# The last feed-forward groups of a two-layer transformer on one core: 256, 128 and 128 tokens in place of 384 and 128

## The chip, the core and the metric

The kernel runs on one core of a Trainium2 chip. A core has engines that work side by side and wait for each other by semaphores: TensorE (PE; its weight loads are listed as PEld), VectorE (DVE), ScalarE (ACT), GpSimd (POOL) and SyncE (SP, which here only issues DMAs). PE writes to PSUM, eight banks of 128 x 512 float32 values; ACT and DVE read PSUM, POOL does not. The metric is the device time of one execution, in microseconds (us).

## The reference

Two identical layers, same weights, over 2048 tokens of width 512; 32 heads of width 16; the feed-forward part is 1792 wide. All inputs and the output are bfloat16.

```python
def _A_ref(x, wqkv, wo):
    q, k, v = split((x @ wqkv), 3, heads=32)             # 32 heads of 16
    scores = einsum("bhqd,bhkd->bhqk", q, k) * 16 ** -0.5
    o = einsum("bhqk,bhkd->bhqd", softmax(scores), v)
    return o.reshape(B, S, D) @ wo
def _B_ref(x, w_gate, w_up, w_down):
    return (gelu_tanh(x @ w_gate) * (x @ w_up)) @ w_down

x = A_x
for layer in (0, 1):
    x = x + _A_ref(layernorm(x), A_wqkv, A_wo)
    x = x + _B_ref(layernorm(x), B_w_gate, B_w_up, B_w_down)
```

(The reference writes the four steps out one after the other, and the head split with a transpose.)

## The kernel before

**Work.** The tokens of a layer are cut into query blocks, `layer_blocks`: four of 512 in layer 0; 512, 512, 512, 256, 128 and 128 in layer 1. A *unit* is one block with one group of four heads; there are 80, each gone through twice.

The *first pass* makes the scores of 128 queries with 512 keys of one head in a PSUM bank (PE, L1791) and DVE reduces one or two banks at once to row maxima (L1806). Some of this is *folded*: PE scores the queries with the difference of two key blocks (L1610), ACT keeps its positive part (L1617), and one special DVE instruction adds the plain scores and takes the maximum (L1801), so that one DVE instruction does two tiles.

The *second pass* makes the scores again with the keys as rows (PE, L1661), with the maximum taken away by a row that four small DMAs put beside the queries (L1189); ACT takes exponentials of one or two banks at once into `SCR` (L1637); PE multiplies them with the values (L1685) into bank 7; ACT copies that out (L1238), POOL or DVE divides by the row sum. A *position* is two tiles of 512 columns of either pass; each pass has 2048 positions over both layers.

After a block's second pass comes its output projection, `outproj`, whose result ACT copies (L1266) for POOL to add to `X` (L1268), or DVE adds at once (L1261). Then the feed-forward part (FFN), `ffn`, for one *group* of tokens, `ffn_groups`: four of 512 in layer 0; 512, 512, 512, 384 and 128 in layer 1. It normalises the group's tokens and turns each 128-token tile by a DMA on SP's queue (L921), then goes through three stages:

- gates: for each of 14 slices of 128 columns, four matmuls as wide as the group (L717), and a gelu on ACT into `HT` (L1353). From the first gate to the last `gel["on"]` is set (L1348 to L1356): no exponential is given out in that time, since gelu and exponential need different ACT tables (`ACT_TABLE_LOAD`); below it is called the *pause*. The first pass goes on in it.
- up-projection: 14 times four matmuls, and the product with `HT`, either by DVE alone (L1363) or by a copy on ACT (L1369) and a product on POOL (L1371).
- down-projection: for each tile of 128 tokens 14 matmuls of 512 columns, then in layer 1 the sum with `X` on DVE (L1389) and a DMA to the output.

The groups hold the buffer `HT` one after another (`locks`). The last group, of 128 tokens, has a name of its own, `HTL`, for the columns from `c0` on (L1319), and takes a *fast* way: its vector work goes to DVE, its transposes through PE, and its gelu table is loaded ahead of its layer norm (L1326). It can only start after the last unit's second pass.

**Order.** No engine decides anything while the kernel runs. A planner in `_build` writes the order of every engine's instructions when the kernel is built. It keeps an estimated clock per engine; tasks such as `outproj` or `ffn` are generators with a due position of the first pass; the main loop at each step gives PE a first-pass tile or pair, second-pass tiles, a PV product, a piece of a task, or, if PE's recent load is low, a filler matmul with zeros (L1830). Semaphore waits are added afterwards from the buffers read and written.

A group's FFN becomes open when its first tile is projected, its gates need all its tiles normalised, and its due position is the end of the block that holds its last token, less 10 (`FDL`; the last group is urgent, L1470 to L1474).

**Constants.** `PLAN` has 132 rows; row k holds for the 16 positions of the first pass from 16k on (L1847). There are 2048 positions, so row 128 holds after the first pass's end, and rows 129 to 131 are never read. The names of the 21 numbers of a row stand in the same line:

```python
SPC, SPLIT, S1C, S2C, OV, LIM, NT, P2B, LAG, LAGT, FL, GL, FX, AHD, DUE, DUEM, PIECE, GP, NPV, PB, OVF = PLAN[stretch[0]]
```

Those that matter most below: `LAGT`: a result is evacuated from PSUM by DVE if the first pass is more than that many positions ahead of the second, else by ACT (`pick`; after the first pass's end always by DVE). `P2B`: which bank pairs the second pass may use in ordinary mode; with 0 none, so that exponentials are single tiles. In *wide* mode pairs are always used; near the end (first pass beyond position 1688) the mode is wide when the second pass is over 10 positions behind and no task piece is open or ready with a due position that has come. After the first pass pairs are used anyway. `S1C`, `S2C`, `SPC`, `SPLIT`, `LIM`, `OV`, `OVF`: when the next pass tile must be given out and how far other work may push it back. `PIECE`, `GP`: how many matmuls of a task, or of a gate, form one piece, counted in 512 columns. `NT`: second-pass tiles given out at once. `DUE`, `DUEM`, `AHD`: what counts as due and as ready.

The lines that the mode and the pairs hang on:

```python
wide = pos["p1"] - pos["p2"] > (LAGE if near_end() else LAG) and not opened and can_p2[0] and not (fresh and min(c.due for c in fresh) < pos["p1"] + DUE)
for b in ((0, 2, 4) if pos["g"] >= len(p1_list) else (3, 5) if wide else ((), (4,), (4, 5))[P2B]):
```

Of the kernel before, what the change touches and what calls it, by code (L numbers as in the profile page):

```python
# [153 lines left out]
]  # L154


# [157 lines left out]
            self.done = True  # L314


def _build(nc, x_in, wqkv, wo, wg, wu, wd, out, layer_blocks=((512, 512, 512, 512), (512, 512, 512, 256, 128, 128)), ffn_groups=((512, 512, 512, 512), (512, 512, 512, 384, 128)),
           n_ahead=6, n_pre=6, S1C=0.45, S2C=0.42, OV=0.3, PD=80, FDUE=20, LIM=-0.05, NT=1, AHD=2.0, DUEM=2, FDL2=0, OPD=12, URG=0.3, ft_tok=512, n_pt=8, n_qt=8, SPLIT=0.15, SPC=0.1, PVC=47, WARM=0.55, WARML=0.42, NPV=7, BOOST=0.0, LAG=62, LAGT=84, GP=2, SING=0, DUE=0, END=360, LAGE=10, FD=205, FDL=-10, QD=32, KD_=16, VD=20, FL=8, FMAX=6, NKD=2, FLOOK=2, FX=0.3, GF=1, NSPL=5, HSPL=0, TSPL=1, HNA=3, TNA=3, PB=1, OVF=0.0, FNP=1, NSG=3, LNT=8, HV=16, TW=0.95, HF=60, VS=14, SO=1.0, SF=1, SP=0, FAST=1, P2B=1, PIECE=2, GL=60, GLE=20, HARD=-1e9, VPARK=60, RUSH=1, XL=1000, NFE=2, NFA=6, LM1=0, T0=0.6, A3=1, DTX=2, DTA=2, T_TP=0.7, T_TPI=2.0, VL=0):
    S = x_in.shape[1]
    D = x_in.shape[2]  # L320
# [13 lines left out]
    with es:  # L334
# [980 lines left out]
        def ffn(la, t0, n, due):  # L1315
            tts = list(range(t0 // 128, (t0 + n) // 128))
            last = la == NL - 1
            fast = FAST and last and t0 + n == S
            c0 = ffn_groups[la][-2] if fast and ffn_groups[la][-2] + n <= ft_tok else 0  # L1319
            hn = "HTL" if c0 else "HT"  # L1320
            yield ("cond", lambda: ao_rec.get(tts[0]) == la)
            while locks.get(hn):
# [118 lines left out]
        for la in range(NL):  # L1441
# [28 lines left out]
            for gi, n in enumerate(ffn_groups[la]):  # L1470
                bi = [i for i, b in enumerate(blocks) if b[0] == la and b[2] <= f0 + n - 1 < b[2] + b[3]][0]
                lastb = gi == len(ffn_groups[la]) - 1
                due = URGENT if lastb and la == NL - 1 else blk_end[bi] + (FDL2 if lastb else FDL if la == NL - 1 else FD)
                add(ffn(la, f0, n, due), due)  # L1474
                f0 += n
# [598 lines left out]
```

## Time and profile before

| what | value |
|---|---|
| median of 3 runs | 2481.18 us (2481.1 to 2481.72) |
| the profiled execution | 2481.77 us, span 2480.0 us |
| granted TensorE clock | 1.00 |
| ACT_TABLE_LOAD at L1353 and at L1637 | 8 and 8, 1283 ns each |
| last tile of the first pass (L1806) ends | 2426.9 us |
| last exponential (L1637) ends | 2459.0 us |

The profile is one execution. Its page gives the busy time of each engine and the chain of work that ended last, followed back from the end; the trace answers further questions: instructions in order of time, groups of instructions in a window (count, busy time, mean of one in ns, idle time of the engine before them and who ended it), and the busy time of every engine in given stretches, where (x n) is the number of instructions. "SCR<-PS" names what is written and what is read. Times in the trace count from the span's start. An instruction's recorded duration overlaps the next one's start a little, so what it costs an engine in a row of its kind is the length of the row divided by the count.

### The profile page before, as it was taken

Reading aid. Unit: us, or ns where it says so; the run is one execution under the profiler, and the core shown is the slowest. Engines: PE = TensorE matmul, PEld = TensorE weight load, DVE = VectorE, ACT = ScalarE, POOL = GpSimd, SP = SyncE. Lnnn points to the kernel's source line nnn. Section 1 sums busy time; section 2 is a strip of 40 time slices with the busy share of each in tenths; the row PEclk is TensorE's granted clock in tenths of the full one; section 3 lists DMA queues with packets and bytes.
Section 4 is the critical chain, followed back from the end, with each engine's and each line's share of the span. In section 5 each row is a group of like instructions: output and inputs, shape, how many; then the busy total and the mean of one; then the engine's idle time right before and its main releaser. Section 6 shows DMA issues by size and latency. Waiting matters only on the chain.

```text
span 2480.0 us, 69071 instructions
## 1 busy us (share of the span) xinstructions
PE 2409.1 (97%) x30004; PEld 1147.4 (46%) x30004; DVE 2382.1 (96%) x3173; ACT 2331.1 (94%) x3415; POOL 810.2 (33%) x1311
## 2 busy tenths in 40 slices
PE   8999999999999999999999999999999999999999
PEld 3444444444434454344434444434544345544655
DVE  8999999999999999999998999999999999999993
ACT  7999998999989999899989999989999999978987
POOL 5121125425433353521333131623116321333520
PEclk9999999999999999999999999999999999999999
DMA  3110000000000001000000000000000000000000
GB/s 94 44 57 15 2 15 12 2 2 15 13 12 2 4 11 23 6 14 11 11 10 2 9 15 5 10 16 8 4 13 15 2 10 3 14 10 12 13 8 10
DMA packets 64816, 34.32 MB, mean 14 GB/s; under 512 B 46848, under 2 KB 63488, under 8 KB 64512
## 3 DMA queue, kind: packets, MB, share of 16 engines
q1 hardware_dynamic: 64512, 29.90, 5.2%
q8 instruction: 235, 3.85, 0.6%
q14 instruction: 69, 0.57, 0.1%
HBM read 10.22 MB, written 2.10 MB: 5 GB/s over the span
## 4 chain that ended last, share of the span: by engine, by line
PE 47%; DVE 33%; ACT 19%; issue 1%; POOL 0%; ACTq 0%
DVE PM L1806 31%; ACT SCR L1637 17%; PE PS L1791 16%; PE PS L717 13%; PE PS L1685 10%; PE PS L1661 4%; PE PS L1830 4%; DVE SCR L1801 1%; ACT SCR L1617 1%; PE PS L1610 0%; PE PS L914 0%; ACT AO L1266 0%; ACT ACCS L1238 0%; ACT L1637 0%; DVE ST L769 0%
## 5 line engine op out<-in xcount | busy, mean ns | idle before, releaser
L1806 DVE TENSOR_REDUCE PM<-PS 128x1 f32<-128x512 f32 (+1 forms) x2507 | 2189.9, 935 | 47.6 <-PE PS L1661 25.1
L1637 ACT ACTIVATE SCR<-PS 128x512 bf16<-128x512 f32 (+1 forms) x2726 | 2005.9, 848 | 45.9 <-PE PS L1661 32.2
L1791 PE MATMUL PS<-KT,QT 32*128 32x512 bf16 x3894 | 1019.3, 384 | 41.3 <-DVE PM L1806 25.2
L1661 PE MATMUL PS<-QT,KT 32*128 32x512 bf16 (+2 forms) x5120 | 919.3, 340 | 2.6 <-ACT SCR L1637 1.7
L1685 PE MATMUL PS<-VP,SCR 128*128 128x51 bf16 (+1 forms) x16384 | 802.9, 187 | 10.1 <-ACT SCR L1637 5.3
L1685 PEld LDWEIGHTS PS<-VP,SCR 128*128 128x128 bf16 x16384 | 574.7, 96 | 473.4 <-issue 395.6
L1791 PEld LDWEIGHTS PS<-KT,QT 32*128 32x128 bf16 x3894 | 243.2, 91 | 526.3 <-DVE PM L1806 298.2
L1830 PE MATMUL PS<-WV,ZER 128*128 128x240 bf16 x2284 | 419.9, 265 | 3.9 <-ACT ACCS L1238 1.9
L1248 POOL TENSOR_TENSOR RL<-ACCS,CM 128x16 f32<-128x16 f32 (+2 forms) x71 | 182.2, 2567 | 485.2 <-ACT ACCS L1238 484.6
L1661 PEld LDWEIGHTS PS<-QT,KT 32*128 32x128 bf16 x5120 | 247.6, 91 | 73.9 <-ACT SCR L1637 44.3
L1830 PEld LDWEIGHTS PS<-WV,ZER 128*128 128x128 bf16 x2284 | 170.0, 96 | 70.0 <-issue 57.3
L1145 POOL TENSOR_TENSOR PM<-PM 128x16 f32<-128x16 f32 (+3 forms) x142 | 32.4, 228 | 425.0 <-DVE PM L1806 410.7
L1371 POOL TENSOR_TENSOR HT<-HT,AO 128x512 bf16<-128x512 bf16 x91 | 105.4, 1161 | 174.0 <-ACT AO L1369 174.0
L1408 POOL TENSOR_TENSOR KD<-KT 128x512 bf16<-128x512 bf16 x80 | 92.2, 1153 | 139.6 <-PE PS L1610 132.8
L1617 ACT ACTIVATE SCR<-PS 128x512 bf16<-128x512 f32 (+1 forms) x143 | 112.1, 787 | 26.3 <-PE PS L1610 25.3
L1801 DVE CUSTOM_DVE_ANT_0 SCR<-PS,SCR 128x512 bf16<-128x512 f32 x202 | 130.1, 686 | 3.2 <-PE PS L1661 1.2
L717 PE MATMUL PS<-XNT,WU 128*128 128x512 bf16 (+2 forms) x504 | 132.2, 357 | 0.0
L717 PE MATMUL PS<-WD,HT 128*128 128x512 bf16 x448 | 130.7, 381 | 0.0
L1268 POOL TENSOR_TENSOR X<-X,AO 128x512 f32<-128x512 f32 x47 | 59.5, 1266 | 199.2 <-ACT AO L1266 199.2
L717 PE MATMUL PS<-XNT,WG 128*128 128x512 bf16 (+2 forms) x504 | 119.9, 358 | 0.7 <-ACT HT L1353 0.7
L1353 ACT ACTIVATE HT<-PS 128x512 bf16<-128x512 f32 (+2 forms) x126 | 68.5, 550 | 43.1 <-PE PS L717 42.3
L717 PEld LDWEIGHTS PS<-XNT,WG 128*128 128x128 bf16 x504 | 37.6, 97 | 57.8 <-issue 33.2
(128 smaller groups left out, 1043.0 us busy)
## 6 DMA issues: line engine op xcount, KB each, us to landing
KT<-SG SPq DMA_DIRECT2D x64, 64.0 KB
QT<-MT SPq DMA_DIRECT2D x244, 1.0 KB
QT<-SG SPq DMA_DIRECT2D x56, 64.0 KB
out_dram<-AO SPq DMA_DIRECT2D x16, 128.0 KB, 1.7
WG<-in_B_w_gate_dram SPq DMA_DIRECT2D x4, 448.0 KB, 5.1
WU<-in_B_w_up_dram SPq DMA_DIRECT2D x4, 448.0 KB, 4.8
WD<-in_B_w_down_dram SPq DMA_DIRECT2D x4, 384.0 KB, 4.6
QT<-MT SPq DMA_DIRECT2D x68, 0.2 KB
```

The source lines that it names most:

```text
L717: ins = e.matmul(out_ap, lhsT=l, rhs=r_, start=(i == 0), stop=(i == n - 1))
L1248: emit("pool", lambda e: e.tensor_tensor(RL[:, s, 0:4 * nq], lsum, AP(CM1, 0, [[1, 128], [0, 4 * nq]]), op=ALU.pow), r=[("ACCS", s), ("CM1 ...
L1371: emit("pool", lambda e, ft=ft, o=o: e.tensor_tensor(HT[:, ft, c0:c0 + n], HT[:, ft, c0:c0 + n], AO[:, o, 0:n], op=ALU.mult), r=[("AO", o) ...
L1408: emit("pool", lambda e: e.tensor_tensor(KD[:, s, :], KT[:, g, ka * 512:(ka + 1) * 512], KT[:, g, kb * 512:(kb + 1) * 512], op=ALU.subtrac ...
L1617: emit("act", lambda e: e.activation(PT[:, s0:s0 + cnt, :], PS[:, bk:bk + cnt, :], ACTF.Relu), r=bks, w=[("PT", s0 + d) for d in range(cnt ...
L1637: emit("act", lambda e: e.activation(dst, src, ACTF.Exp, scale=DH ** -0.5), r=[BK[bk + i] for i in range(cnt)], w=[("PT", i) for i in slot ...
L1661: ins = e.matmul(bank(bk)[:, i * n:(i + 1) * n], lhsT=KT[32 * j:32 * j + 32, g, kt * 128:(kt + 1) * 128], rhs=QT[32 * j:32 * j + 32, s, 0: ...
L1685: ins = e.matmul(acc, lhsT=PT[:, slot, i * n + qt * 128:i * n + (qt + 1) * 128], rhs=AP(VP, (kt * H + 4 * g + j) * 17, [[NTT * H * 17, 128 ...
L1791: ins = e.matmul(bank(b), lhsT=QT[32 * j:32 * j + 32, s, qt * 128:(qt + 1) * 128], rhs=KT[32 * j:32 * j + 32, g, kb * 512:(kb + 1) * 512], ...
L1801: emit("dve", lambda e, i=i, b=b, sl=sl: e.tensor_tensor_reduce(PT[:, sl, :], bank(b), PT[:, sl, :], 1.0, -3.0e38, ALU.add, ALU.max, po[:, ...
L1806: emit("dve", lambda e: e.tensor_reduce(po, PS[:, bs[0]:bs[0] + cnt, :], axis=AX.X, op=ALU.max), r=bks, w=[("PM", sm) + h[1:] for h in hs] ...
L1830: return e.matmul(PS[:, b, NACC:512], lhsT=ZER[:, :], rhs=WV[:, 0, 0:512 - NACC], start=(b != 7), stop=(b != 7), skip_group_check=True)
```

## The change

Two things. In layer 1 the FFN group of 384 tokens (1536 to 1919) becomes two, of 256 (1536 to 1791) and 128 (1792 to 1919). Both still use `HT` one after the other; the last 128 tokens are a fast group as before, and the line that gives its first column `c0` is written otherwise (512 - 128 = 384; before, the preceding group's 384). The due position of the 256 group is 1920 - 10, that of the middle 128 group 1984 - 10, as that of the 384 group was.

And 39 of PLAN's 132 rows, 93 to 131, have new numbers; they hold from position 1488 of the first pass on, which is from about 1743 us. Rows 0 to 92 and every default of `_build` but `ffn_groups` stay. A few of the rows, with their number at the end of the line here:

```diff
@@ PLAN @@
-    (0.4, 0.1, 0.55, 0.52, 0.0, -0.05, 3, 0, 70, 76, -2, 80, 0.7, 2.0, 10, 2, 2, 1, 7, 3, -0.1),      99
+    (0.2, 0.1, 0.75, 0.42, 0.0, 0.0, 2, 2, 70, 76, -2, 80, 0.7, 1.0, 10, 2, 2, 1, 7, 3, 0.1),         99
...
-    (0.3, 0.1, 0.55, 0.52, 0.5, -0.05, 2, 0, 30, 20, -17, 50, 0.4, 2.5, -10, 2, 1, 1, 14, 2, 0.0),    114
+    (0.3, 0.05, 0.55, 0.52, 0.5, -0.05, 2, 2, 30, 20, 8, 50, 0.4, 2.5, -10, 14, 1, 1, 14, 1, 0.0),    114
...
-    (0.1, 0.3, 0.45, 0.42, 0.1, 0.0, 2, 1, 14, 116, 13, 100, 0.3, 3.5, 0, 2, 2, 1, 7, 1, -0.05),      116
-    (0.15, 0.1, 0.55, 0.42, 0.3, -0.05, 2, 0, 22, 84, 13, 20, 0.3, 4.0, 0, 6, 2, 4, 9, 2, 0.0),       117
-    (0.15, 0.1, 0.45, 0.42, 0.3, -0.05, 2, 0, 22, 10, 8, 20, 0.3, 4.0, 0, 6, 2, 4, 9, 2, 0.0),        118
-    (0.35, 0.05, 0.55, 0.42, 0.2, -0.1, 2, 0, 22, 76, 8, 100, -0.2, 3.0, 0, 10, 1, 1, 11, 1, 0.1),    119
-    (0.15, 0.1, 0.45, 0.12, 0.5, 0.0, 2, 0, 22, 10, 8, 20, 0.3, 4.0, 0, 10, 1, 4, 9, 2, 0.2),         120
-    (0.2, 0.1, 0.55, 0.42, 0.3, -0.05, 2, 1, 22, 84, 8, 20, 0.4, 4.0, 0, 6, 2, 4, 14, 2, 0.0),        121
-    (0.2, 0.1, 0.55, 0.32, 0.3, -0.05, 2, 0, 22, 84, 8, 20, 0.3, 4.0, 10, 6, 2, 4, 5, 2, 0.2),        122
-    (0.35, 0.05, 0.65, 0.42, 0.2, -0.05, 2, 0, 62, 76, 8, 100, -0.3, 4.0, -5, -14, 1, 1, 11, 1, 0.1), 123
-    (0.35, 0.05, 0.55, 0.42, 0.7, -0.05, 2, 0, 62, 84, 8, 100, -0.3, 2.5, 20, 6, 1, 4, 11, 1, 0.0),   124
-    (0.35, 0.05, 0.55, 0.42, 0.2, -0.05, 2, 0, 62, 84, -2, 100, -0.3, 2.5, 20, 6, 1, 4, 11, 1, 0.05), 125
-    (0.3, 0.15, 0.75, 0.42, 0.3, -0.05, 3, 0, 5, 76, 8, 60, -0.2, 1.5, 15, -6, 2, 4, 14, 2, 0.0),     126
-    (0.3, 0.15, 0.75, 0.42, 0.0, -0.1, 2, 0, 14, 0, 8, 60, -0.3, 1.5, -10, -14, 2, 4, 3, 3, -0.05),   127
-    (0.2, 0.05, 0.65, 0.42, 0.3, -0.05, 1, 1, 30, 116, 8, 40, 0.7, 3.0, 15, 10, 1, 4, 14, 3, -0.1),   128
+    (0.15, 0.1, 0.55, 0.42, 0.3, -0.05, 2, 1, 30, 84, 8, 20, 0.3, 4.0, 0, 6, 2, 4, 9, 2, 0.0),        116
+    (0.15, 0.1, 0.55, 0.42, 0.3, -0.05, 2, 0, 70, 84, 8, 20, 0.3, 4.0, 0, 6, 2, 4, 9, 2, 0.0),        117
+    (0.15, 0.1, 0.15, 0.42, 0.3, -0.05, 2, 0, 22, 10, 8, 20, 0.2, 4.0, 0, 6, 2, 4, 9, 2, 0.0),        118
+    (0.15, 0.1, 0.15, 0.42, 0.3, -0.05, 2, 0, 22, 10, 8, 20, 0.2, 4.0, 0, 6, 2, 4, 9, 2, 0.0),        119
+    (0.15, 0.1, 0.15, 0.42, 0.3, -0.05, 2, 0, 22, 10, 13, 20, 0.2, 4.0, 0, 6, 2, 4, 9, 2, 0.0),       120
+    (0.2, 0.0, 0.65, 0.42, 0.3, -0.1, 2, 2, 70, 84, 8, 0, 0.3, 2.5, -5, 2, 2, 1, 7, 4, 0.1),          121
+    (0.3, 0.3, 0.55, 0.42, 0.1, 0.0, 3, 0, 22, 76, -30, 50, -0.3, 1.0, -5, -6, 2, 3, 3, 2, 0.2),      122
+    (0.15, 0.1, 0.45, 0.22, 0.0, -0.05, 2, 2, 70, 84, 8, 100, 0.2, 1.0, 0, 6, 2, 3, 9, 1, 0.0),       123
+    (0.35, 0.15, 0.75, 0.62, 0.3, -0.05, 3, 0, 5, 84, 8, 80, 0.3, 1.0, 15, -6, 2, 3, 3, 1, 0.0),      124
+    (0.3, 0.15, 0.75, 0.42, 0.3, -0.05, 3, 0, 5, 76, -2, 60, -0.2, 1.5, 15, -6, 2, 4, 14, 2, 0.0),    125
+    (0.05, 0.15, 0.75, 0.42, 0.1, -0.1, 3, 1, 14, 10, 13, 60, -0.3, 1.0, -10, -14, 1, 4, 3, 3, -0.05),126
+    (0.35, 0.05, 0.55, 0.52, 0.5, -0.05, 2, 0, 30, 20, 8, 50, 0.4, 2.5, -10, 2, 1, 1, 14, 2, 0.0),    127
+    (0.35, 0.05, 0.55, 0.52, 0.5, -0.05, 2, 0, 30, 20, 8, 50, 0.4, 2.5, -10, 2, 1, 1, 14, 2, 0.0),    128
...
@@ def _build @@
-  ffn_groups=((512, 512, 512, 512), (512, 512, 512, 384, 128)),
+  ffn_groups=((512, 512, 512, 512), (512, 512, 512, 256, 128, 128)),
...
@@ def ffn @@
-            c0 = ffn_groups[la][-2] if fast and ffn_groups[la][-2] + n <= ft_tok else 0
+            c0 = ft_tok - n if fast else 0
```

Among the new rows, P2B is 2 in rows 99, 111 to 114, 121 and 123 and 1 in rows 93, 116 and 126; before it was 1 in rows 116, 121 and 128 and 0 in the others from 93 to 127. LAGT is 40 or less in the new rows 93 to 96, 114, 118 to 120 and 126 to 128; before in 93, 103, 111, 112, 114, 118, 120 and 127.

More of the change, by code (lines that the diff above doesn't have):

```diff
@@ L314, in step, with _build @@
             self.done = True
-def _build(nc, x_in, wqkv, wo, wg, wu, wd, out, layer_blocks=((512, 512, 512, 512), (512, 512, 512, 256, 128, 128)), ffn_groups=((512, 512, 512, 512), (512, 512, 512, 384, 128)),
+def _build(nc, x_in, wqkv, wo, wg, wu, wd, out, layer_blocks=((512, 512, 512, 512), (512, 512, 512, 256, 128, 128)), ffn_groups=((512, 512, 512, 512), (512, 512, 512, 256, 128, 128)),
            n_ahead=6, n_pre=6, S1C=0.45, S2C=0.42, OV=0.3, PD=80, FDUE=20, LIM=-0.05, NT=1, AHD=2.0, DUEM=2, FDL2=0, OPD=12, URG=0.3, ft_tok=512, n_pt=8, n_qt=8, SPLIT=0.15, SPC=0.1, PVC=47, WARM=0.55, WARML=0.42, NPV=7, BOOST=0.0, LAG=62, LAGT=84, GP=2, SING=0, DUE=0, END=360, LAGE=10, FD=205, FDL=-10, QD=32, KD_=16, VD=20, FL=8, FMAX=6, NKD=2, FLOOK=2, FX=0.3, GF=1, NSPL=5, HSPL=0, TSPL=1, HNA=3, TNA=3, PB=1, OVF=0.0, FNP=1, NSG=3, LNT=8, HV=16, TW=0.95, HF=60, VS=14, SO=1.0, SF=1, SP=0, FAST=1, P2B=1, PIECE=2, GL=60, GLE=20, HARD=-1e9, VPARK=60, RUSH=1, XL=1000, NFE=2, NFA=6, LM1=0, T0=0.6, A3=1, DTX=2, DTA=2, T_TP=0.7, T_TPI=2.0, VL=0):
```

78 rows, old and new, of the table PLAN are left out of this document.

## The prediction

> **What bounds the kernel now.** I read the page first, then the chain of waits near the end, then the stretches between the last two feed-forward (FFN) groups, then the counts of instructions in them. The page:
>
> ```profile
> span 2480.0 us, 69071 instructions
> PE 2409.1 (97%) x30004; PEld 1147.4 (46%) x30004; DVE 2382.1 (96%) x3173; ACT 2331.1 (94%) x3415; POOL 810.2 (33%) x1311
> PE 47%; DVE 33%; ACT 19%; issue 1%; POOL 0%; ACTq 0%
> ```
>
> DVE and ACT are both nearly full, so an average decides nothing; the end does. The chain's last pieces, and four stretches (length, then busy PE, PEld, DVE, ACT, POOL; the first is used far below):
>
> ```profile
> 2410.74 0.32 PE PS L1791 x2
> 2411.06 0.76 PE PS L717 x4
> ...
> 2438.32 6.38 ACT SCR L1637 x7
> ...
> 2461.13 5.61 PE PS L717 x26
> ...
> 2467.71 9.40 PE PS L717 x126
> ```
>
> ```profile
> 1290.00:1380.00 90.00, 89.21 (x991) 37.20 (x990) 80.24 (x110) 86.01 (x160) 30.59 (x36) 1.00 0.03 6
> 2203.26:2400.91 197.65, 190.68 (x3166) 107.82 (x3164) 189.11 (x242) 188.75 (x304) 78.88 (x161) 1.00 0.05 10
> 2400.91:2419.67 18.76, 18.23 (x113) 7.52 (x113) 18.23 (x24) 9.44 (x16) 0.29 (x1) 1.00 0.01 1
> 2427.00:2459.00 32.00, 31.84 (x583) 19.51 (x582) 7.23 (x18) 31.72 (x44) 1.33 (x5) 1.00 0.01 3
> ```
>
> From 2427 to 2459 ACT works without a gap at exponentials, while DVE, whose first pass is over, stands idle for 24.8 of 32 us. What is left to ACT there:
>
> ```profile
> L1637 ACT ACTIVATE SCR<-PS 128x1024 bf16<-128x1024 f32 x30 | 28.8, 1042 | 0.1
> L1637 ACT ACTIVATE SCR<-PS 128x512 bf16<-128x512 f32 x8 | 4.8, 624 | 0.2 <-PE PS L1661 0.2
> ```
>
> A position of either pass is two 512-column tiles, so 30 + 8/2 = 34 positions stand between the passes. After them a tail of 21 us (last output projection, layer norm, last 128-token FFN) goes through PE. So the end is: ACT's last exponential, plus 21 us. What the change adds to ACT's way there is paid in full; DVE has room.
>
> The row 2400.91:2419.67 is the pause: the gelus of the 384-token group hold the exponentials up from one table load to the other, 18.76 us in which ACT is busy for 9.44.
>
> **The change part by part.** Its time comes from ACT's stream:
>
> ```profile
> 2214.98 7.39 ACT L1637 ACTIVATE SCR<-PS 128x512 bf16<-128x512 f32 x14
> ...
> 2326.94 0.62 ACT L1266 ACTIVATE AO<-PS 128x512 f32<-128x512 f32 x1
> ...
> 2390.48 0.62 ACT L1266 ACTIVATE AO<-PS 128x512 f32<-128x512 f32 x1
> ...
> 2400.91 1.28 ACT L1353 ACT_TABLE_LOAD   x1
> 2404.46 0.49 ACT L1353 ACTIVATE HT<-PS 128x384 bf16<-128x384 f32 x1 [2.27 <-PE PS L717]
> ...
> 2417.88 0.49 ACT L1353 ACTIVATE HT<-PS 128x384 bf16<-128x384 f32 x1 [0.16 <-PE PS L717]
> 2418.39 1.28 ACT L1637 ACT_TABLE_LOAD   x1
> 2419.68 7.95 ACT L1637 ACTIVATE SCR<-PS 128x512 bf16<-128x512 f32 x14
> ...
> 2438.19 7.54 ACT L1637 ACTIVATE SCR<-PS 128x1024 bf16<-128x1024 f32 x8
> ```
>
> ```profile
> 2332.35 3.35 SPq L921 DMA_TRANSPOSE XNT<-XN  x2
> ```
>
> The attention of the 256-token block is projected at 2327 and its two normalised tiles are transposed by 2335.7; the 384 group must wait for its third tile (2390.48). So the new 256 group can start its pause near 2336, and the new middle 128 group near 2401. No DMA is added: each tile is transposed once, as before.
>
> (a) Two pauses for one. In the old pause one gate tile takes 0.76 us of PE (four matmuls of 384 columns) and a first-pass pair 0.32: 14 × 1.08 = 15.1, and 3.7 around them. For 256 columns: 14 × (0.51 + 0.32) = 11.6, + 3.7 = 15.3. For 128, I let two gates (0.25 each) go per pair: 7 × 0.82 = 5.7, + 3.7 = 9.4. Together 24.7 against 18.76: **+6.0**. Gelus by width:
>
> ```profile
> L1353 ACT ACTIVATE HT<-PS 128x512 bf16<-128x512 f32 x98 | 58.5, 597 | 33.3 <-PE PS L717 32.5
> L1353 ACT ACTIVATE HT<-PS 128x384 bf16<-128x384 f32 x14 | 6.9, 491 | 9.3 <-PE PS L717 9.3
> L1353 ACT ACTIVATE HT<-PS 128x128 bf16<-128x128 f32 x14 | 3.2, 278 | 0.5 <-PE PS L717 0.5
> ```
>
> Lower bound, were ACT never to wait: four loads 5.1, 14 × 0.384 (256 lies midway between 278 and 491) and 14 × 0.278, 14.4 in all: -4.4. Upper, one pair per gate: 14 × 0.57 + 3.7 = 11.7 for 128, 27.0 in all: +8.2. I stay with +6.0, nearest to the old pause's own rhythm.
>
> The two more table loads are 2 × 1.28 of this. The row 2418.39 shows the load 0.02 us after a gelu, and the exponential 0.01 us after the load. The Trainium skill ("ScalarE: Activation LUTs", What ACT_TABLE_LOAD costs) adds a drain and counts about 2.66 us a switch, and asks to batch calls by table set, which speaks against this change. By its figure the sum would be some 2.8 us higher; this trace shows no such drain.
>
> (b) The up-projection's results. Before, the 384 group's fall on DVE, after ACT is the only bound. The 256 group's come after 2336 + 15.3 = 2351. Where in the plan is that? The passes' counts, 2195.4 to 2282.6, then 2344 to 2384.1, then to the end:
>
> ```profile
> L1806 DVE TENSOR_REDUCE PM<-PS 128x2 f32<-128x1024 f32 x42 | 51.3, 1221 | 3.5 <-PE PS L1661 2.5
> L1806 DVE TENSOR_REDUCE PM<-PS 128x1 f32<-128x512 f32 x45 | 30.3, 681 | 0.2 <-PE PS L1661 0.2
> ```
>
> ```profile
> L1806 DVE TENSOR_REDUCE PM<-PS 128x2 f32<-128x1024 f32 x20 | 24.4, 1222 | 1.2 <-PE PS L1661 0.5 <-PE PS L1791 0.2
> L1806 DVE TENSOR_REDUCE PM<-PS 128x1 f32<-128x512 f32 x25 | 16.8, 681 | 0.1
> ```
>
> ```profile
> L1806 DVE TENSOR_REDUCE PM<-PS 128x2 f32<-128x1024 f32 x23 | 27.1, 1210 | 0.9 <-PE PS L1791 0.5 <-PE PS L1661 0.3
> L1806 DVE TENSOR_REDUCE PM<-PS 128x1 f32<-128x512 f32 x16 | 10.8, 679 | 0.2 <-PE PS L1661 0.2
> L1801 DVE CUSTOM_DVE_ANT_0 SCR<-PS,SCR 128x512 bf16<-128x512 f32 x1 | 0.7, 681 | 0.0
> ```
>
> The last gives 23 + 8 + 1 = 32 positions (a folded one is a whole position), so 2384.1 is position 2016 of 2048, and 2344 is about 1984: rows 124 and 125 of the plan rule in between. The new ones have LAGT 84 and 76, and the passes stand far less apart (34 at the end): the copies go to ACT. A copy holds ACT up for 0.47 us at 512 columns and, less 256 × 0.83 ns (the gelus' slope), 0.26 at 256:
>
> ```profile
> 2204.72 0.62 ACT L1369 ACTIVATE AO<-PS 128x512 f32<-128x512 f32 x1
> 2205.19 2.59 ACT L1637 ACTIVATE SCR<-PS 128x512 bf16<-128x512 f32 x5
> ```
>
> 14 × 0.26 = **+3.7** (0 if all fall on DVE). POOL multiplies them, with 119 us free of 198.
>
> (c) Single exponentials. Row P2B = 0 forbids pairs while overdue FFN work waits. A single holds ACT for 7.39/14 = 0.528 us, a pair for 7.54/8 = 0.943: 0.057 per tile. After the last 512 group (2195.4 to 2282.6), and from 2344 to 2384.1:
>
> ```profile
> L1637 ACT ACTIVATE SCR<-PS 128x512 bf16<-128x512 f32 x134 | 70.7, 613 | 6.0 <-PE PS L1661 5.2
> ```
>
> ```profile
> L1637 ACT ACTIVATE SCR<-PS 128x1024 bf16<-128x1024 f32 x36 | 34.2, 1058 | 0.7 <-PE PS L1661 0.2
> ```
>
> The 512 group kept 134 tiles single; half its work keeps 67. These were pairs, and new rows 124 and 125 have P2B = 0: 67 × 0.057 = **+3.8** (0 to that).
>
> (d) Evacuations that new thresholds of 10 (rows 119, 126) move to DVE: two of the 512 group's copies, one projected tile, one query: 3 × 0.47 + 0.3 = **-1.7** (0 to that).
>
> (e) In the tail the 26 matmuls from 2461.13 are mostly the 384 group's down-projection, queued ahead of the last transposes. Without them the layer norm ends 0.6 us earlier: **-0.6**.
>
> (f) The other constants. Seven new rows have P2B = 2; by my count along the trace about 61 of the singles of the stretch lie under four of them. As pairs: 61 × 0.057 = **-3.5**. Bounds: ACT's 8.9 idle us in 2203.26:2400.91 gone, -8.9; or, nearest row of a stretch that fits badly, 1290 to 1380, where DVE idles 9.8 and ACT 4 of 90 us, +10.
>
> (g) At nothing: 112 narrower matmuls more on PE, covered by filler matmuls (L1830, x2284, in the page); the first column c0, 384 before and after; the new wait of the middle 128 group for the first one's buffer, which lies in the order written at build time, with no engine's queue behind it.
>
> Sum: 6.0 + 3.7 + 3.8 - 1.7 - 0.6 - 3.5 = +7.7. The profiled execution took 2481.8, 0.6 above the median: 2481.8 + 7.7 - 0.6 = **2489**, 0.3% slower. Its own range: the distances to the lower ends are 10.4, 3.7, 3.8 and 5.4, to the upper ones 2.2, 1.7 and 13.5; they will not all come together, so I take half the root of the summed squares, 6.4 down and 6.9 up: 2483 to 2496.
>
> **Rivals.** (1) Faster: pairs. The changed stretch holds this many single and paired exponentials (1743 to 2427):
>
> ```profile
> L1637 ACT ACTIVATE SCR<-PS 128x1024 bf16<-128x1024 f32 x367 | 344.7, 1088 | 3.7 <-PE PS L1661 2.6
> L1637 ACT ACTIVATE SCR<-PS 128x512 bf16<-128x512 f32 x442 | 235.2, 616 | 11.8 <-PE PS L1661 8.8
> ```
>
> If the new rows pair 300 of the singles instead of 61, ACT gains 239 × 0.057 = 13.6 more and the time is 2475. It is faster by over 5 us from (7.7 + 5)/0.057 = 223 more pairs on. For it: ACT ends last, with DVE idle for 24.8 us to catch up into. Against: new rows 102 to 108, 115 and 117 to 120, where most singles lie, keep P2B = 0.
>
> (2) The early start does not come: the 256 group's gates run as late as the 384 group's. Then copies fall on DVE, exponentials after the first pass are pairs, and the tail keeps its down-projections: 6.0 - 1.7 - 3.5 = +0.8, 2482. For it: one piece of the plan can hold a chain back; against: tiles ready at 2335.7.
>
> (3) The new rows fit as badly as those from 1290 to 1380: +10 in place of -3.5, 2502.
>
> **How the numbers follow.** 0.2% (5 us) is about what a measurement of this kernel can tell from no change. Forecast 0.46, of which 0.06 lies within 0.2%; rival 1 0.33, of which 0.02 only gets that far; rival 2 0.09; rival 3 0.12. Faster 0.31; same 0.06 + 0.02 + 0.09 = 0.17; slower 0.40 + 0.12 = 0.52. The range 2471 to 2500 leaves out the far ends of rivals 1 and 3.
>
> **What would show it.** Nine table loads for gelus at L1353 and nine back at L1637; pauses near 2336 of 15 us and near 2401 of 9 us; 14 copies of 256 columns at L1369; singles between 2351 and 2384; the last exponential near 2467 instead of 2459, and more than 34 positions between the passes when DVE's first pass ends. It is wrong if the last exponential ends before 2459: then look for pairs in place of singles, or for pauses at ACT's own pace.

## The result, and the profile after

The changed kernel takes 2490.36 us (median of 5 runs, 2490.0 to 2491.03) against 2481.57 us of the kernel before on the same chip: a ratio of 1.0035, 95% interval 1.0024 to 1.0046, 0.35% slower. The forecast was 2489. The page of the changed kernel:

```profile
span 2488.6 us, 69441 instructions
PE 2419.4 (97%) x30146; PEld 1161.2 (47%) x30146; DVE 2378.7 (96%) x3182; ACT 2341.5 (94%) x3461; POOL 812.0 (33%) x1324
PE 47%; DVE 32%; ACT 19%; issue 1%; POOL 0%; POOLq 0%; ACTq 0%
```

Both PE and ACT have 10 us more to do, and the shares by engine say nothing. The stretches behind the last 512-token group are (length, then busy PE, PEld, DVE, ACT, POOL, then the granted clock, the DMA share and GB/s):

```profile
2206.87:2335.75 128.88, 126.41 (x1904) 64.47 (x1903) 114.85 (x148) 122.83 (x215) 44.43 (x90) 1.00 0.06 12
2335.75:2350.07 14.32, 13.19 (x115) 7.83 (x112) 13.91 (x18) 7.92 (x16) 4.28 (x12) 1.00 0.01 1
2350.07:2418.94 68.87, 68.10 (x1145) 43.34 (x1145) 54.51 (x76) 64.69 (x127) 28.47 (x68) 1.00 0.05 12
2418.94:2427.16 8.22, 7.54 (x84) 4.56 (x84) 8.02 (x16) 6.34 (x17) 0.62 (x2) 1.00 0.01 2
2427.16:2451.03 23.87, 23.87 (x439) 17.33 (x438) 22.43 (x40) 23.20 (x51) 2.68 (x7) 1.00 0.01 3
2451.03:2468.65 17.62, 17.55 (x327) 11.16 (x325) 1.81 (x8) 17.56 (x24) 1.04 (x4) 1.00 0.04 10
```

The second and fourth rows are the two new pauses, 14.32 and 8.22 us. Between them, in the third row, DVE is busy for only 54.51 of 68.87 us: the first pass stands still for 14 us (before, DVE idled 8.5 us in all the 198 us ahead of the pause), while PE is busy for all but 0.77 us. The first pass ends at 2451.03 (before: 2426.87). In the last row ACT alone counts, as it did in 2427:2459 before. ACT's groups from 2206 to the end, and its first loads and last exponential:

```profile
L1637 ACT ACTIVATE SCR<-PS 128x512 bf16<-128x512 f32 x298 | 158.9, 613 | 5.8 <-PE PS L1661 3.7 <-PE PS L1791 0.2
L1637 ACT ACTIVATE SCR<-PS 128x1024 bf16<-128x1024 f32 x67 | 64.2, 1046 | 3.2 <-PE PS L1661 2.9
L1353 ACT ACTIVATE HT<-PS 128x256 bf16<-128x256 f32 x14 | 5.4, 383 | 6.4 <-PE PS L717 6.0
L1369 ACT ACTIVATE AO<-PS 128x256 f32<-128x256 f32 x10 | 4.2, 416 | 0.0
L1369 ACT ACTIVATE AO<-PS 128x128 f32<-128x128 f32 x5 | 1.6, 318 | 0.0
```

```profile
2335.75 1.28 ACT L1353 ACT_TABLE_LOAD   x1
...
2348.79 1.28 ACT L1637 ACT_TABLE_LOAD   x1
...
2418.94 1.28 ACT L1353 ACT_TABLE_LOAD   x1
...
2425.88 1.28 ACT L1637 ACT_TABLE_LOAD   x1
...
2467.96 0.69 ACT L1637 ACTIVATE SCR<-PS 128x512 bf16<-128x512 f32 x1
```

The last exponential ends at 2468.65 instead of 2459.02: 9.6 us later, and the tail behind it is 20.0 instead of 21.0 us. That is the span's whole difference, 8.6.

The same in another reading. When the first pass is over, the second needs about 0.95 us for each position that it still lags: 32.15 us for 34 positions before, 17.62 for 18.5 after. The first pass ends 24.2 us later, the second is then 15.5 positions nearer, worth 14.7 us; 9.5 us stay. So the loss is made where both passes run, and the stretch to ask is the one between the pauses. From 2353.5 to 2402 (plan rows 124 and 125) the changed kernel shows these groups:

```profile
L1637 ACT ACTIVATE SCR<-PS 128x512 bf16<-128x512 f32 x85 | 45.3, 615 | 1.9 <-PE PS L1661 1.1 <-PE PS L1791 0.2
L717 PE MATMUL PS<-WD,HT 128*128 128x512 bf16 x28 | 8.4, 381 | 0.0
L717 PE MATMUL PS<-XNT,WU 128*128 128x256 bf16 x48 | 7.3, 274 | 0.0
L1830 PE MATMUL PS<-WV,ZER 128*128 128x240 bf16 x7 | 1.7, 265 | 0.0
```

All exponentials but one are single, the whole down-projection and nearly all of the up-projection of the 256 group stand here, and of the filler matmuls (L1830) seven are left. In the kernel before, rows 124 and 125 (2343.9 to 2384.1) held 60 of them:

```profile
L1830 PE MATMUL PS<-WV,ZER 128*128 128x240 bf16 x60 | 10.7, 265 | 1.5 <-ACT ACCS L1238 1.2 <-DVE PM L1806 0.3
```

By the counts of L1806, L1801 and L1637 these two rows take 48.3 us for 32 positions of the first pass and 42 of the second, where before they took 40.1 for 32 and 40. At the pace of before, 74 positions would take 41.2 us: an estimate of 7 of the 9.5 us for these two rows. The chain of waits in this stretch, by line, first after (2353 to 2403), then before (2353 to 2400.9):

```profile
by line: PE PS L1661 28.6%; PE PS L1685 27.0%; PE PS L717 25.8%; PE PS L1791 14.3%; DVE PM L1806 2.5%; PE PS L1830 1.6%; issue 0.3%
```

```profile
by line: ACT SCR L1637 23.4%; DVE PM L1806 18.8%; PE PS L1685 18.4%; PE PS L1661 14.4%; PE PS L1791 13.3%; PE PS L1830 10.9%; PE PS L717 2.3%; issue 1.1%; ACT AO L1266 1.0%; ACT ACCS L1238 0.5%
```

Before, the chain went from engine to engine, with fillers as slack; after, 97% of it lies on PE, a quarter on projections (L717), nearly all of them the group's own. This is what the prediction left at nothing.

### The profile page after: what moved, and what is told of

It is laid out like the page before. It is cut to its first block, busy times and chain, and to the rows that moved or that the text cites. A ratio compares the mean times of both kernels' runs of the same rounds, so it can differ in the third digit from the quotient of the medians.

```text
span 2488.6 us, 69441 instructions
## 1 busy us (share of the span) xinstructions
PE 2419.4 (97%) x30146; PEld 1161.2 (47%) x30146; DVE 2378.7 (96%) x3182; ACT 2341.5 (94%) x3461; POOL 812.0 (33%) x1324
## 4 chain that ended last, share of the span: by engine, by line
PE 47%; DVE 32%; ACT 19%; issue 1%; POOL 0%; POOLq 0%; ACTq 0%
DVE PM L1806 30%; ACT SCR L1637 18%; PE PS L1791 15%; PE PS L717 13%; PE PS L1685 11%; PE PS L1661 5%; PE PS L1830 4%; DVE SCR L1801 1%; ACT SCR L1617 1%; PE PS L1610 1%; ACT L1637 0%; PE PS L914 0%; ACT AO L1266 0%; ACT ACCS L1238 0%; ACT HT L1353 0%
## 5 line engine op out<-in xcount | busy, mean ns | idle before, releaser
L1806 DVE TENSOR_REDUCE PM<-PS 128x2 f32<-128x1024 f32 (+1 forms) x2496 | 2183.4, 936 | 57.1 <-PE PS L1661 34.0
L1637 ACT ACTIVATE SCR<-PS 128x512 bf16<-128x512 f32 (+1 forms) x2746 | 2011.2, 844 | 46.0 <-PE PS L1661 32.3
L1830 PE MATMUL PS<-WV,ZER 128*128 128x240 bf16 x2314 | 422.3, 266 | 3.5 <-ACT SCR L1637 2.1
L1830 PEld LDWEIGHTS PS<-WV,ZER 128*128 128x128 bf16 x2314 | 173.7, 96 | 72.2 <-issue 58.7
L1371 POOL TENSOR_TENSOR HT<-HT,AO 128x512 bf16<-128x512 bf16 (+2 forms) x101 | 108.4, 1076 | 195.1 <-ACT AO L1369 195.0
L1801 DVE CUSTOM_DVE_ANT_0 SCR<-PS,SCR 128x512 bf16<-128x512 f32 x208 | 133.6, 686 | 2.9 <-PE PS L1661 0.9
L717 PE MATMUL PS<-XNT,WU 128*128 128x512 bf16 (+2 forms) x560 | 131.9, 338 | 0.1
L717 PE MATMUL PS<-WD,HT 128*128 128x512 bf16 x448 | 131.7, 381 | 0.0
L717 PE MATMUL PS<-XNT,WG 128*128 128x512 bf16 (+2 forms) x560 | 120.4, 339 | 0.2
L1353 ACT ACTIVATE HT<-PS 128x512 bf16<-128x512 f32 (+2 forms) x140 | 70.5, 512 | 42.2 <-PE PS L717 41.2
L717 PEld LDWEIGHTS PS<-XNT,WG 128*128 128x128 bf16 x560 | 41.0, 98 | 55.3 <-issue 31.2
```

Source lines behind the costliest of these rows:

```text
L717: ins = e.matmul(out_ap, lhsT=l, rhs=r_, start=(i == 0), stop=(i == n - 1))
L1371: emit("pool", lambda e, ft=ft, o=o: e.tensor_tensor(HT[:, ft, c0:c0 + n], HT[:, ft, c0:c0 + n], AO[:, o, 0:n], op=ALU.mult), r=[("AO", o) ...
L1637: emit("act", lambda e: e.activation(dst, src, ACTF.Exp, scale=DH ** -0.5), r=[BK[bk + i] for i in range(cnt)], w=[("PT", i) for i in slot ...
L1801: emit("dve", lambda e, i=i, b=b, sl=sl: e.tensor_tensor_reduce(PT[:, sl, :], bank(b), PT[:, sl, :], 1.0, -3.0e38, ALU.add, ALU.max, po[:, ...
L1806: emit("dve", lambda e: e.tensor_reduce(po, PS[:, bs[0]:bs[0] + cnt, :], axis=AX.X, op=ALU.max), r=bks, w=[("PM", sm) + h[1:] for h in hs] ...
L1830: return e.matmul(PS[:, b, NACC:512], lhsT=ZER[:, :], rhs=WV[:, 0, 0:512 - NACC], start=(b != 7), stop=(b != 7), skip_group_check=True)
```

## Experiments

Four theories were set against each other. Theory 1 is the prediction's: what is added to ACT's way to its last exponential is paid in full. Theory 2: the first pass's stall is the price, because the last block's query projections come late behind the group's overdue work. Theory 3: PE's time is the price. Theory 4: the group's up and down work takes PSUM banks and so splits the exponentials. All ratios are to the kernel before on the same chip, with 95% intervals.

**Each half of the change alone.**

```diff
  groups_alone: the changed kernel, PLAN rows of the kernel before
  consts_alone: the kernel before, PLAN rows of the changed kernel
```

> The new FFN groups (256, 128, 128) with all 132 old PLAN rows. Theory 1 (ACT sets the end and the split is what ACT pays for): two pauses for one cost about 3.8 us as in the changed kernel's trace (14.3 + 8.2 against 18.8), the 256 group's up copies fall on ACT under the old rows 124 and 125 too (LAGT 84) for about 3 us, singles some 1 to 3, the tail gives 1 back: 2487 to 2490. Rival (the constants are the cost, the split is free): within 2 us of 2481.5.

> The old FFN groups (384, 128) with the new PLAN rows. Theory 1: the new rows cost nothing by themselves; in the changed kernel's trace the second pass is 8 to 9 positions further at 2284 us than before, so the time is between 2473 (all of that kept) and 2482. Rival (the constants are the cost): about 2490, as the changed kernel.

The groups alone: 2500.31 us, 1.0079 [1.0065, 1.0093]. The constants alone: 2483.34, 1.0006 [0.9998, 1.0015], no change that can be told. So the split costs 18.8 us under the old rows and 7.0 under the new ones (2490.36 - 2483.34): the constants are worth nothing by themselves, and beside the split they bring 10.0 us (2500.31 to 2490.36). Under the old rows DVE waits thus from 2351 to 2404 (us in all, times, longest):

```profile
DVE HT L1363 <- PE PS L717: 11.5, 8, 2.4
DVE PM L1806 <- PE PS L1661: 5.3, 4, 4.0
```

Eight of the 256 group's 14 up-projections are multiplied on DVE here and wait 11.5 us for PE at the head of its queue, with the reductions of the first pass behind them. With the new rows it is four, which wait 0.7 us. The threshold LAGT is not what moved them: it is 84 in the old rows 124 and 125, 84 and 76 in the new ones, and the passes stand at most 48 positions apart there. `pick` also gives a result to DVE when no first-pass tile is ready. Both kernels with the split end the first pass at 2451.0; what differs is how far the second then lags, 28.5 positions against 18.5, and at 0.95 us each that is 9.5 of the 10.0 us.

**Pairs instead of singles, and copies on DVE instead of ACT.**

```diff
  pairs: the changed kernel, P2B 0 -> 2 in rows 124 and 125
  copies_dve: the changed kernel, LAGT 84, 84, 76 -> 10 in rows 123 to 125
```

> The changed kernel with P2B = 2 in rows 124 and 125. Its 84 single exponentials there become up to 42 pairs. Theory 1, singles as I costed them (0.041 to 0.057 us a tile): 3.4 to 4.8 us less, 2486 to 2487. Rival (singles cost nothing, since the gaps between them are set by PE): 2490, no change.

> The changed kernel with LAGT = 10 in rows 123, 124 and 125, so that the 256 group's up copies go to DVE, which idles there. Theory 1 (10 copies hold ACT for 0.295 us each): 3 us less, about 2487.5. Rival (ACT is not the bound there, DVE's idle time in rows 125 and 126 is the sign of another): no change or more, since DVE gets 10 x 0.4 us more work.

Pairs: 2496.94, 1.0061 [1.0048, 1.0073], so 6.6 us slower than the changed kernel although the 84 singles of the two rows fell to 23 with 27 pairs. The time went into ACT waiting: busy for 22.60 of the 26.5 us of row 125, and for 6.12 of the middle 128 group's pause, which grew from 8.22 to 12.83 us:

```profile
2374.10:2400.60 26.50, 25.86 (x436) 15.47 (x436) 21.25 (x29) 22.60 (x32) 8.59 (x21) 1.00 0.09 21
...
2420.24:2433.07 12.83, 11.49 (x120) 6.79 (x118) 12.69 (x16) 6.12 (x16) 0.29 (x1) 1.00 0.01 1
```

Copies on DVE: 2516.94, 1.0133 [1.0110, 1.0155], the slowest of all. From 2376 to 2432 DVE stood waiting for two down-projections:

```profile
DVE AO L1389 <- PE PS L717: 22.5, 2, 15.7
```

In this run the granted clock fell to 0.79 over 13.8 us, so not all of its 26.6 us over the changed kernel are the copies'. In both runs less work for ACT in rows 124 and 125 did not shorten the time. But each also gave every engine a new order, so neither shows alone that ACT is not the bound; the run with less work for ACT, below, keeps the order.

**The query projections earlier.** The last block's query projections are given a due time 110 positions ahead instead of 32, under the old and the new rows.

```diff
-                add(qproj(u), first_p1[u] - QD, True)
+                add(qproj(u), first_p1[u] - (QD if units[u][1] < len(blocks) - 1 else 110), True)
```

> The new FFN groups with the old PLAN rows (2500.3 so far), and the last block's query projections due 110 positions ahead of their use in place of 32, so before the 256 group's FFN (due 1910). In the trace of the new groups with old rows these projections came at 2378 to 2404 us, after that group's up and down matmuls, and DVE idled 19 us waiting for queries. Theory 2 (the overdue FFN work holds the last block's queries up, the first pass ends late and ACT then lacks work): DVE's idle time in row 125 goes below 4 us, the first pass ends 15 to 20 us earlier, and the time is 2488 to 2493. Theory 1 alone (only ACT's own added work counts; DVE's stall is free): the first pass ends earlier but the time stays at 2499 to 2501.

> The changed kernel (2490.4) with the same earlier due positions for the last block's query projections. Theory 2: DVE's 7 + 7 idle us of rows 125 and 126 go, the time falls by 3 to 7 us, to 2483 to 2487. Theory 1 alone: 2490, no change.

Old rows: 2500.15, 1.0085 [1.0071, 1.0099]; the first pass ended at 2441.7 instead of 2451.0, DVE's idle time in row 125 fell from 19.4 to 4.2 us, and the last exponential came at 2478.0 as before (2478.2). New rows: 2495.66, 1.0057 [1.0045, 1.0069], 5.3 us slower than the changed kernel. Under the old rows, a first pass that ends 9 us earlier takes nothing off the end, which speaks against Theory 2. The stall was moved rather than taken away, though: DVE's idle time rose from 0.7 to 10.5 us in row 127, and under the new rows from 6.7 to 10.1 in row 126.

**The lead before the groups.** At 2284 us the second pass of the changed kernel is 8.5 positions ahead of where it was before. The kernel before with the new rows up to 120 only:

```diff
  mix: the kernel before, rows 0 to 120 of the changed kernel, rows 121 to 128 its own
```

> The old groups with the new rows up to 120 and the old rows from 121 on. With the new rows the second pass was 8 to 9 positions further at 2284 us, and with new row 121 the first pass then lost 8 us. If that lead is worth time when the old rows follow: 2473 to 2478, faster than before. If the lead is only the first pass's own lateness (lag 34 instead of 44 at the same position): 2481 to 2484, no gain.

2487.31, 1.0023 [1.0014, 1.0032], 5.7 us slower: the lead alone is worth nothing. The first pass ends 9 us later here than in the kernel before (2435.9), and the lead is lost again in the rows that follow.

**The price of a table switch.** In the kernel before, when the second pass is at position 2030, four pairs of a Gelu and an Exp of one column are put into ACT's stream, all other order the same (the line in short):

```diff
+  for f in (ACTF.Gelu_apprx_tanh, ACTF.Exp) * 4:          # once, when pos["p2"] >= 2030
+      sch.op("act", lambda e, f=f: e.activation(KBIAS[:, 1:2], CM05[:, 0:1], f), ...)
```

> The kernel before, every engine's order the same, with four extra pairs of a gelu and an exponential of one column on ACT after position 2030 of the second pass, where ACT alone is busy: eight more table loads. If ACT sets the end there and a switch costs only its load: 8 x 1.28 + 8 x about 0.15 = 11 to 12 us more, 2493. If each switch also drains for 1.38 us, as the Trainium skill (ScalarE: Activation LUTs, What ACT_TABLE_LOAD costs) has it: 22 to 23 us more, 2504. If something else than ACT sets the end: less than 5 us more.

2500.91, 1.0077 [1.0065, 1.0089]: 19.3 us for eight loads. ACT's rows, and the stretches around them:

```profile
2441.99 1.28 ACT L1639 ACT_TABLE_LOAD   x1
2443.28 0.20 ACT L1639 ACTIVATE KBIAS<-CM 128x1 f32<-128x1 f32 x1
2443.50 1.28 ACT L1639 ACT_TABLE_LOAD   x1
...
2453.99 2.83 ACT L1637 ACTIVATE SCR<-PS 128x1024 bf16<-128x1024 f32 x3
```

```profile
2438.00:2442.00 4.00, 4.00 (x81) 2.42 (x80) 1.18 (x3) 3.98 (x7) 0.29 (x1) 1.00 0.02 4
2442.00:2454.00 12.00, 1.28 (x25) 0.61 (x21) 0.56 (x1) 11.79 (x17) 0.00 (x0) 0.70 0.00 0
...
2457.00:2461.00 4.00, 4.00 (x47) 2.00 (x43) 1.18 (x3) 2.50 (x4) 0.29 (x1) 0.50 0.00 0
...
2472.00:2478.00 6.00, 6.00 (x96) 3.62 (x94) 0.56 (x1) 5.36 (x7) 0.27 (x2) 0.83 0.01 3
```

A load and its instruction take 1.51 us, one behind the other, 12.0 in all and no drain between. The other 7 us come after them: PE, which was busy for 1.28 of those 12 us, goes on at half its clock, and now ACT waits for PE (busy 2.50 of 4.00 us). Here, with nothing but the second pass left, ACT's time is paid in full, as the prediction held.

**Less work for ACT, and less for PE, in the place where the change puts it.** The order of all engines is that of the changed kernel; part of the 256 group's feed-forward is left out (the edits in short):

```diff
  act_less, the 256 group only:
-    e.activation(HT[:, ft, c0:c0 + n], bank(bg)[:, 0:n], ACTF.Gelu_apprx_tanh)
+    e.activation(HT[:, ft, c0:c0 + 8], bank(bg)[:, 0:8], ACTF.Copy)
-    e.activation(AO[:, o, 0:n], bank(bu)[:, 0:n], ACTF.Copy)
+    e.activation(AO[:, o, 0:8], bank(bu)[:, 0:8], ACTF.Copy)
  pe_less, up and down matmuls of the 256 group only:
-    for i in idx:
+    for i in list(idx)[-1:]:
```

> The changed kernel, order of all engines the same, but the 256 group's 14 activations are issued as Copy over 8 columns (so neither its Gelu nor the two table loads around it run) and its up copies on ACT are issued over 8 columns: part of the 256 group's feed-forward is not computed. Theory 1 (time taken from ACT on its way to the last exponential is paid in full): less by the two loads, 2.56 us, by ten copies some 0.1 us shorter each, 1.0, and by up to 1.3 us of the 14 activations: 2485.5 to 2487. Theory 3 (PE is the engine that the 256 group crowds): PE has the same instructions, so no change, 2490 within 1 us.

> The changed kernel, but of the 256 group's up matmuls one of four is issued (14 for 56) and of its down matmuls one of two (14 for 28): part of its feed-forward is not computed; ACT and DVE have the same instructions in the same order, PE the same order. It takes 42 x 0.107 + 14 x 0.215 = 7.5 us from PE between 2351 and 2407 us. Theory 3 (PE is full there, fillers almost gone: 9 of them between 2350 and 2402): 3 to 7 us less, 2483 to 2487. Theory 1: PE's matmuls lie beside ACT's exponentials, so no change, 2490 within 1 us.

Less for ACT: 2490.58, 1.0034 [1.0022, 1.0047], the changed kernel's time. Its stretches, and below them the changed kernel's over the same times:

```profile
2335.80:2350.10 14.30, 13.42 (x114) 7.95 (x112) 13.89 (x17) 3.37 (x16) 4.50 (x13) 1.00 0.01 2
2353.50:2402.00 48.50, 47.64 (x808) 30.87 (x810) 40.74 (x55) 45.77 (x101) 21.96 (x48) 1.00 0.04 9
```

```profile
2335.80:2350.10 14.30, 13.17 (x115) 7.81 (x112) 13.89 (x18) 7.90 (x17) 4.23 (x12) 1.00 0.01 1
2353.50:2402.00 48.50, 48.28 (x815) 30.89 (x813) 40.69 (x56) 46.64 (x101) 22.08 (x48) 1.00 0.04 9
```

ACT is busy for 4.5 us less in the pause and 0.9 less behind it, and every later event stands within 0.4 us of where it stood: the first pass ends at 2451.26 (2451.03). In the pause DVE is full (13.89 of 14.30), behind it PE is. With this order, ACT's time there is worth nothing, and Theory 1 falls for this place. (The order was written out for the longer ACT work, and the exponentials still stand behind the gates in it: what the length of a pause costs the second pass is not tested by this. A plan made anew could have used the gap. That was not tried.)

Less for PE: 2501.53, 1.0080 [1.0066, 1.0094], 11 us slower with 7.5 us of matmuls taken away. Its clock:

```profile
2350.00:2395.00 45.00, 43.62 (x518) 28.34 (x521) 28.16 (x37) 35.71 (x73) 18.83 (x39) 0.52 0.01 2
...
2400.00:2410.00 10.00, 9.46 (x178) 6.47 (x179) 9.70 (x15) 9.87 (x20) 3.63 (x9) 1.00 0.11 28
```

The granted clock is 0.52 over the 45 us from 2350, where the changed kernel has 1.00 throughout. At half clock the comparison is no test of Theory 3 as it was meant; it does show that the stretch gets longer when PE is slower: 32 positions of the first pass took 60.2 us at half clock and 48.3 at the full one.

**The group's up and down work later.** After its gate the 256 group waits for the first pass; in the second kernel the middle 128 group also gets columns and a lock of its own.

```diff
  late_new, in ffn, behind the gates:
+            if (la, t0) == (1, 1536):
+                yield ("cond", lambda: pos["p1"] >= 2040)
  own_columns: the same with 2012, and
-            hn = "HTL" if c0 else "HT"
+            c0 = 256 if last and (t0, n) == (1792, 128) else c0
+            hn = "HTL" if fast and c0 else "HTM" if c0 else "HT"
```

> The changed kernel, but after its gate the 256 group waits until the first pass is at position 2040 of 2048 with its up and down work, as the 384 group's came after the first pass in the kernel before. Two pauses remain. Theory 3: PE is freed of 12 us of matmuls while both passes run and takes them when the first pass is over, so some 5 us less than the changed kernel, near 2485. Theory 1: the pauses, copies and single exponentials are still there, so 2490 within 3 us; the copies may even go to DVE, which stands idle after the first pass, 3 us less.

> The changed kernel, but the 256 group waits after its gate until the first pass is at position 2012 of 2048 with its up and down work, and the middle 128 group has columns 256 to 383 of HT and a lock of its own, so that it need not wait for the 256 group (as it must in the run in which that group waited to position 2040, whose tail after the last exponential grew from 20.0 to 30.7 us). In the order as issued, single exponentials after the last 512 group fall from 298 to 232, up and other copies through AO from 19 to 10, and PE's work behind the last scores is 10.0 us as in the changed kernel (9.8). Theory 4 (up and down work between the two passes takes PSUM banks, so that exponentials go single and both passes wait for each other; pauses and loads are not what costs): the last exponential comes between 2452.3 and 2468.7, near 2458, and the tail stays near 20: 2480, between 2475 and 2484. Theory 3 (PE's time is full wherever the work stands): the work only moves, so 2486 to 2490.

Waiting to 2040: 2485.78, 1.0016 [1.0007, 1.0025], 4.6 us faster than the changed kernel. The pause near 2335 is the same 14.32 us, with the same two loads and the same 14 gelus. The stretch behind it, and its chain by line from 2353 to 2393 (in this kernel L1639 is the exponential, L1808 the reduction, L1832 the filler):

```profile
2353.50:2402.00 48.50, 46.55 (x923) 31.33 (x923) 46.87 (x60) 46.59 (x64) 18.71 (x47) 1.00 0.04 8
```

```profile
by line: ACT SCR L1639 28.6%; DVE PM L1808 19.8%; PE PS L1793 15.7%; PE PS L1687 15.5%; PE PS L1663 12.1%; PE PS L1832 8.2%; PE PS L717 1.7%; issue 1.3%
```

DVE is busy for 46.87 instead of 40.69 us, fillers are back, and the chain is as mixed as it was before. Rows 124 and 125 take 39.8 us for 32 positions of the first pass and 39 of the second, where the changed kernel took 48.3 for 32 and 42. The last exponential ends at 2452.3: 16.4 us ahead of the changed kernel and 6.7 ahead of the kernel before. But the tail is 30.7 us, since the middle 128 group now waits for the columns of the 256 group, and PE has both to do behind the last exponential.

This run does not tell PE from ACT by itself, because Theory 1's terms moved as well. The middle group's gelus came after the last exponential (from 2460.8), so only one pause is left on the way to it, and L1353 loads eight gelu tables, not nine. The singles of rows 124 and 125 fell from 84 to 9, and no copy of an up-projection stands in these rows.

With columns of its own and 2012: 2488.64, 1.0029 [1.0018, 1.0041]. The first pass ended 12 us earlier than in the changed kernel (2439.06), 66 singles fewer were issued, the tail was 20.4, and rows 124 and 125 took 39.5 us, as with the wait to 2040. But the middle group's pause then lay across the end of the first pass (2433.5 to 2444.0, so that its last 5 us had no first pass to lie beside), and the last exponential ended at 2466.5. Theory 4 wanted 2480 and misses; Theory 3, that the work only moves, had 2486 to 2490. No kernel of these twelve beats the kernel before.

## Why the prediction was right

Direction and size were right (2489 against 2490.36), the mechanism only in part: the sum names the right work, but where it put the price the runs found none. That the total came within 1.4 us is luck: the copies and singles that it adds (7.5 us) are not what the runs found paid, and the matmuls that it puts at nothing stand where some 7 us were lost.

- **"What the change adds to ACT's way there is paid in full."** Right behind the first pass's end, where the switches cost at least their 12 us and the 0.95 us a position hold. Wrong where the change adds it: 5.4 us taken from ACT's busy time between 2336 and 2402, in the same order, gave back nothing (2490.58). This is the step that failed. In its place the stretch between the pauses has PE on 97% of its chain of waits.
- **(a) Pauses, +6.0.** The lengths came out: 14.32 for 15.3 and 8.22 for 9.4, so +3.8. The place of the first did too (2335.75), but not that of the second: 2418.94 instead of 2401, because the tile that it waits for was added to `X` at 2409.9 and not, as before, at 2392.4. What a pause costs need not be its length, since the first pass goes on in it; no run measures it.
- **(b) Copies, +3.7.** Ten of 256 columns in 256's stretch and five of 128 hold ACT up for 2.95 + 0.84 = 3.8 us. The size is right, the count is not: of the 14 copies forecast ten came, since `pick` gave DVE the other four. The run with less work for ACT shows that the ten were not paid for.
- **(c) Singles, +3.8.** They came (84 in rows 124 and 125, 67 expected). With pairs, and the order that came with them, the time rose by 6.6 us: the singles were not what could be saved there.
- **(d) Evacuations, -1.7.** ACT's 512-column copies (L1369) fell from 21 to 16, 2.3 us, one projected tile fewer (L1266) is some 0.5, and query projections (L736) 0.3: about -3.1.
- **(e) Tail, -0.6.** Measured -1.0.
- **(f) Constants, -3.5.** By themselves +1.8 us with an interval that holds zero; 64 singles fewer stand in rows 98, 99, 114 and 123 by the trace, for 61 counted, but by themselves the rows keep no lead. Beside the split they bring 10.0 us: there the lead is kept, 10 positions when the first pass ends.
- **(g) "112 narrower matmuls ... covered by filler matmuls", at nothing.** By the chain of waits this missed the term behind most of the difference, though no run isolates it. Not the number of matmuls matters but their place: the 384 group did 12 of its 14 up-projections and all its down-projections after the first pass, when that pass's matmuls were gone; the 256 group does them while both passes run, and there the fillers ran out (seven in 48.5 us).
- **The rivals.** Pairs in place of singles (2475) came to about the 61 of the forecast, not 300. The early start did come, at 2335.75. Badly fitting new rows (2502) did not come: it is the old rows that fit the split badly, 2500.31.
- **"More than 34 positions between the passes when the first pass ends."** Wrong: 18.5. The first pass was held up, not the second; of all the signs named this was the one that could tell ACT from PE as the bound, and it fell the other way. The last exponential, 2468.65 for 2467, came out by a sum of another kind.

So the cause is argued and not shown: the chain of waits, the missing fillers and the run with less work for ACT point to PE. What stays open is how much of the 7 to 9 us is PE's time itself and how much the fixed order in which its queue serves both passes, or the banks of Theory 4. The run that took PE's work away also took its clock, and the runs that moved the work moved pauses, copies and singles with it. It also stays open whether a plan made for late up- and down-projections would keep the 6.7 us by which the last exponential came earlier, without the longer tail.

## What to carry to other kernels

When several engines are over 90% busy, price a piece of work that moves by the engine that is on the chain in the stretch it moves to, and count there what slack (here fillers) is left; the engine that ends last is the price only in the stretch where it is alone. A sum can be right in total and wrong in its terms: shorten one term in place, in the same order, and see whether the end moves.

## What was not expected of the hardware

PE's clock answers to work taken away. After 12 us in which PE was busy for 1.28, the granted clock was 0.50 until about 2474, 20 us after the loads were over, although PE's rows are full (4.00 of 4.00 us) from 2457 on; the eight loads cost 19.3 us and not 12.0. The Trainium skill ("TensorE: Matmul & The Clock Gate", Part 1: The HAM clock gate) names half rate after an idle window of some 3.4 us and full rate after a busy one of the same length. The fall agrees with this trace: PE's last matmul ended at 2443.3, and the clock fell at about 2446.9. The way back took several times as long here; in that time ACT waited 0.5 to 0.7 us for PE before almost every exponential. Why it took so long stays open.

In the run with 42 up and 14 down matmuls fewer it took far less. PE's gaps around the end of the pause were 0.89, 0.33 and 0.30 us (in the changed kernel 0.56 and 0.33, and where the up work waits to 2040, 0.76 and 0.33; in both the clock held); the granted clock then fell at about 2352 and stayed near half for 45 us, with PE's rows nearly full. So with 7.5 us less work for PE the kernel was 11 us slower (7 to 16 us over its four executions). That the gaps are what tips the clock is not shown. That matmuls which compute nothing can be worth their time is what this run suggests; a kernel without its fillers was not tried.
